# Padding the rows of the Q, K and gate-logit tiles to 256 bytes, and computing the gates' exp in place

## The chip, the cores and the metric

The kernel runs on one core of one Trainium2 chip. The metric is the device time of one execution, in microseconds (us). Most executions of one kernel on one chip lie within some 0.3% of each other.

## The reference, cut to what matters

A gated linear recurrence (8 heads of 48, 4 batches, 768 steps), then a mixture of four experts over the 3072 rows that come out of it.

```python
f = 1.0 / (1.0 + np.exp(-f_logit))
for t in range(S):                                  # S = 768
    state = f[:, :, t, :, None] * state + einsum('bhd,bhe->bhde', k[:, :, t], v[:, :, t])
    y[:, :, t] = einsum('bhd,bhde->bhe', q[:, :, t], state)
x = y.transpose(0, 2, 1, 3).reshape(3072, 384)
p = domain_probs / (domain_probs.sum(-1, keepdims=True) + 1e-09)
for e in range(4):                                  # w1: 384 x 1024, w2: 1024 x 384
    out += p[:, e:e + 1] * (np.maximum(x @ w1[e], 0.0) @ w2[e])
```

## The kernel before

The recurrence is done in 6 chunks of 128 steps. A small planner fixes the order of the instructions on every engine before anything is emitted, and puts 34 filler matmuls into gaps to keep the tensor engine's clock up. Inputs are loaded per chunk, in the first chunk one batch at a time: 128 partitions x 8 heads, thus 1024 rows of 48 floats (192 bytes) per load. Each of the inputs f (gate logits), q and k has four tiles, called slots here. A slot holds two batches: in chunk 0 batches 0 and 1 go to slot 0 and batches 2 and 3 to slot 1, chunk 1 uses slots 2 and 3, and so on around.

```python
shapes = {
    "f": ([T, 2 * H, D], FP32), "q": ([T, 2 * H, D], FP32), "k": ([T, 2 * H, D], FP32), ...
    "ex": ([T, 2 * H, D], FP32), ...                # T = 128, H = 8, D = 48
}
def load(c, nm, b, n):
    if (c, nm) == (0, "v"):                         # issued by GpSimd, casts to bf16
        ins[c, nm, b] = nc.gpsimd.dma_start(out=tl("vb", c, b), in_=srcs[nm][c, :, b * H:(b + n) * H, :])
        if b < 2:
            after(ins[c, nm, b], ins[v_gate[b]])    # v_gate = [(0, "k", 1), (0, "k", 2)]
        return
    ins[c, nm, b] = nc.sync.dma_start(out=tl(nm, c, b // 2)[:, hh(b, n), :], in_=srcs[nm][c, :, b * H:(b + n) * H, :])
    ...
def load_w(i, e, which, ks, cols):                  # weights, issued by GpSimd after v
    ...
    if i == w_last:
        after(ins["w", i], ins[1, "k", 0])

def gate1(c, b, n):
    nc.scalar.activation(out=tl("ex", c, b)[:, 0:n * H], in_=tl("f", c, b // 2)[:, hh(b, n), :], func=AF.Exp, scale=-1.0)
def gate2(c, b, n):
    ...
    nc.scalar.activation(out=g[:, hh(b, n), 0:D], in_=tl("ex", c, b)[:, 0:n * H], func=AF.Ln, bias=1.0)

# order of the first loads: letter and batch
"f0 k0 q0 f1 k1 q1 f2 f3 k2 q2 v0 k3 q3 v1 v2".split()
```

The v loads of the first chunk are issued by GpSimd only when the k loads of batches 1 and 2 have landed. And the weight pieces are issued on the same engine after the v loads, so a late k load of batch 2 delays the weights too.

Of the kernel before, what the change touches and what calls it, by code (L numbers as in the profile page):

```python
# [8 lines left out]
FP32 = mybir.dt.float32  # L9
BF16 = mybir.dt.bfloat16  # L10
AF = mybir.ActivationFunctionType
# [91 lines left out]
def kernel(  # L103
# [11 lines left out]
    nc = tc.nc  # L115
    B, H, S, D = q.shape
    assert (B, H, S, D) == (4, 8, 768, 48)
    T = 128
# [3 lines left out]
    P2 = 64  # L122
# [12 lines left out]
    wk = ctx.enter_context(tc.tile_pool(name="wk", bufs=1))  # L135
    PS = bass.MemoryType.PSUM
    ps = ctx.enter_context(tc.tile_pool(name="ps", bufs=1, space=PS))
    rooms = {"ps_m": 4, "ps_t": 4, "f": 4, "q": 4, "k": 4, "v": 4, "ex": 2, "gp": 4, "e": 3, "qk": 7,
             "vb": 7, "egs": 8, "QK": 4, "AT": 2, "yb": 2, "xT": 2, "h": 2, "o": 6}
    P = Plan(rooms)  # L140

# [13 lines left out]
    for nm, nb in (("gp", 2), ("qk", 2)):  # L155
        for i in range(rooms[nm]):
            t = pads[nm, i] = const.tile([T, nb, H, P2], BF16, name=f"{nm}{i}")
            nc.vector.memset(t[:, :, :, D:P2], 0.0)
    for i in range(rooms["e"]):
# [5 lines left out]
        out=mask01, in_=mask01, compare_op=ALU.is_ge, fill=0.0,  # L165
# [5 lines left out]
    for i in range(2):  # L171
        t = const.tile([MP, B, NP, 2 * D], BF16, name=f"sb{i}")
# [14 lines left out]
    for nm, a in (("f", f_logit), ("q", q), ("k", k), ("v", v)):  # L187
        srcs[nm] = a.rearrange("b h (c t) d -> c t (b h) d", t=T)
    ins = {}
    tiles = {}  # L190
    shapes = {
        "f": ([T, 2 * H, D], FP32), "q": ([T, 2 * H, D], FP32), "k": ([T, 2 * H, D], FP32), "v": ([T, 2 * H, D], FP32),
        "ex": ([T, 2 * H, D], FP32), "egs": ([128, 16], FP32), "vb": ([T, H, D], BF16),
        "QK": ([128, 2, NP, T], BF16), "AT": ([T, 2, NP, T], BF16), "yb": ([T, HD], BF16),
        "xT": ([128, KD, NT], BF16), "h": ([128, KF, NT], BF16), "o": ([128, Din], FP32),
        "cs": ([T, 512], FP32), "tp": ([128, 2, NP, T], BF16), "A": ([T, NP, T], FP32), "y": ([T, 512], FP32),
# [3 lines left out]
    def tl(kind, *key):  # L200

        if (kind, key) not in tiles:
            room = kind if kind in rooms else "ps_m" if kind in ("hp", "op", "pp") else "ps_t"
            slot = P.slot[(room, kind) + key if room.startswith("ps_") else (room,) + key]
            if room in ("gp", "qk", "e"):
                tiles[kind, key] = pads[room, slot]
            else:
                shape, dt = shapes[kind]
                pool = ps if room.startswith("ps_") else wk
                tiles[kind, key] = pool.tile(shape, dt, name=f"{room}{slot}")  # L210
        return tiles[kind, key]

    def after(later, earlier):
# [7 lines left out]
    def hh(b, n=1):  # L221
        return slice((b % 2) * H, (b % 2 + n) * H)

    def copy(eng, out, in_):
        if eng == "ACT":
            nc.scalar.copy(out=out, in_=in_)  # L226
        else:
            engines[eng].tensor_copy(out=out, in_=in_)
# [33 lines left out]
        nc.vector.tensor_tensor(out=pn, in0=tl("pp"), in1=psm.unsqueeze(1).broadcast_to([T, E, NR]), op=ALU.mult)  # L262

    def gate1(c, b, n):
        nc.scalar.activation(out=tl("ex", c, b)[:, 0:n * H], in_=tl("f", c, b // 2)[:, hh(b, n), :], func=AF.Exp, scale=-1.0)  # L265

    def gate2(c, b, n):
        g = tl("gp", c, b // 2).rearrange("t b h d -> t (b h) d")
        nc.scalar.activation(out=g[:, hh(b, n), 0:D], in_=tl("ex", c, b)[:, 0:n * H], func=AF.Ln, bias=1.0)  # L269

    def pe_cs(c, b):
        g, cs = tl("gp", c, b // 2)[:, b % 2], tl("cs", c, b)
# [134 lines left out]
    ld = {}  # L407
# [15 lines left out]
    for i, x in enumerate("f0 k0 q0 f1 k1 q1 f2 f3 k2 q2 v0 k3 q3 v1 v2".split()):  # L423
        nm, b = x[0], int(x[1])
# [30 lines left out]
    def attention(c, slot, gran):  # L455
        G, X, Y, GS, ET, VB = {}, [], [], [], {}, {}
        more = c < C - 1
        for b0 in range(0, B, gran):
            p, d, half = slot(b0, 0) - 0.5, 0.43 if gran == 1 else 0.84, b0 // 2
            g1 = P.add(f"gate1 {c}.{b0}", {"ACT": d}, lambda e, b0=b0: gate1(c, b0, gran), p,  # L460
                       deps=[ld[c, "f", b0 + i] for i in range(gran)], takes=[("ex", c, b0)], frees=[("f", c, half)])
            g2 = P.add(f"gate2 {c}.{b0}", {"ACT": d}, lambda e, b0=b0: gate2(c, b0, gran), p + 0.1,
                       deps=[g1], takes=[("gp", c, half)], frees=[("ex", c, b0)])
            for b in range(b0, b0 + gran):
                G[b] = g2
        for b in range(B):
            s = lambda k: slot(b, k)
            half = b // 2
# [4 lines left out]
                       deps=[G[b]], takes=[pt_("cs")], lag=0.2, frees=[("gp", c, half)])  # L473
            ex = P.add(f"exps {c}.{b}", {"ACT": 0.98 if c else 0.82}, on(exps), s(0) + 0.1, deps=[cs],
                       takes=[("e", c, b)] + ([("egs", c, b)] if c == 0 else []), frees=[pt_("cs")])
            GS.append(P.add(f"egs {c}.{b}", {"POOL": 0.8}, on(dma_egs), s(10), deps=[ex], takes=[("egs", c, b)],
                            frees=[("e", c, b)], lag=2.8) if c and more else None)
            pe = {"DVE": 0.47} if c == 0 and b == B - 1 else {"DVE": 0.47, "POOL": 1.36} if c == 0 else None
            qm = P.add(f"q {c}.{b}", pe or ({"DVE": 0.8} if (c, b) < (1, 2) else {"POOL": 1.1}), one(product, 0), s(4) - 0.2,
                       deps=[ex, ld[c, "q", b]], takes=[("qk", c, b)], frees=[("q", c, half), ("e", c, b)])  # L480
            km = P.add(f"k {c}.{b}", pe or ({"DVE": 0.5} if (c, b) < (1, 2) else {"POOL": 1.0}), one(product, 1), s(4) - 0.1,
                       deps=[ex, ld[c, "k", b]], takes=[("qk", c, b)], frees=[("k", c, half), ("e", c, b)])
            vb = ld[0, "v", b] if c == 0 else P.add(f"v {c}.{b}", {"POOL": 0.5, "ACT": 0.52} if c == 1 else {"POOL": 0.5}, one(cast_v), s(4),
                       deps=[ld[c, "v", b]], takes=[("vb", c, b)], frees=[("v", c, half)])
            if (c, b) < (1, 2):
                tq = P.add(f"tpq {c}.{b}", {"PE": 0.22}, on(pe_tp, 0), s(4), deps=[qm],
                           takes=[pt_("tp")], frees=[("qk", c, b)], lag=0.2)
                tk = P.add(f"tpk {c}.{b}", {"PE": 0.22}, on(pe_tp, 1), s(4) + 0.01, deps=[km],
                           takes=[pt_("tp")], frees=[("qk", c, b)], lag=0.2)
                parts = [(slice(0, 2), [tq, tk])] if c or b < B - 1 else [(slice(j, j + 1), [tj]) for j, tj in enumerate((tq, tk))]  # L490
                et = [P.add(f"ev_tp {c}.{b}", {"DVE": 0.69, "ACT": 1.05} if c else {"DVE": 0.6, "ACT": 0.92} if len(parts) == 1 else {"DVE": 0.35, "ACT": 0.49},
                            lambda e, b=b, js=js: copy(e, tl("QK", c, b)[0:MP, js], tl("tp", c, b)[0:MP, js]), s(4) + 0.1,
                            deps=ds, takes=[("QK", c, b)], frees=[pt_("tp")]) for js, ds in parts]
            else:
                et = [P.add(f"tp {c}.{b}", {"DMA": 1.8}, on(dma_tp), s(4), deps=[qm, km], takes=[("QK", c, b)],
                            frees=[("qk", c, b)], lag=2.5)]
# [4 lines left out]
        for bs in pairs:  # L501
            at = P.add(f"at {c}.{bs[-1]}", {"PE": 0.43 if len(bs) == 1 else 0.66}, lambda e, bs=bs: [pe_at(c, b) for b in bs], slot(bs[-1], 7),
                       deps=[t for b in bs for t in ET[b]], takes=[("ps_t", "A", c, b, r) for b in bs for r in range(2)], lag=0.2,
                       frees=[("QK", c, b) for b in bs])
            for b in bs:
                AT_[b] = at
        for b in range(B):
# [3 lines left out]
            at, vb = AT_[b], VB[b]  # L511
            eA = [P.add(f"ev_at{r} {c}.{b}", {"DVE": 0.7 if c else 0.62}, on(ev_at, r), s(7) + 0.1 + 0.1 * r, deps=[at],
                        takes=[("AT", c, b)], frees=[pt_("A", r)]) for r in range(2)]
            y = P.add(f"y {c}.{b}", {"PE": 0.4 if c else 0.28}, on(pe_y), s(11), deps=eA + [vb, kvdone.get((c - 1, b))],
                      takes=[pt_("y")], frees=[("QK", c, b), ("AT", c, b), ("vb", c, b)], lag=0.2)
# [4 lines left out]
                        lambda e, b=b, ks=ks: copy(e, tl("yb", c, b)[:, cs_(ks)], tl("y", c, b)[:, cs_(ks)]), s(11) + 0.1,  # L520
                        deps=[y], takes=[("yb", c, b)], frees=[pt_("y")]) for ks in parts]
            if (c, b) < (1, 2):
                xdone[c, b] = []
                for ks, eyk in zip(parts, ey):
                    xt = P.add(f"xt {c}.{b}", {"PE": 0.17}, on(pe_xt, ks), s(13), deps=[eyk],
                               takes=[pt_("xp", ks.start)], frees=[("yb", c, b)], lag=0.2)
                    xdone[c, b].append(
                        P.add(f"ev_xt {c}.{b}", {"ACT": 0.48, "DVE": 0.4} if c else {"ACT": 0.4, "DVE": 0.3} if len(parts) == 1 else {"ACT": 0.3, "DVE": 0.25},
                              lambda e, b=b, ks=ks: copy(e, tl("xT", c)[:, ks, b * T:(b + 1) * T], tl("xp", c, b, ks.start)[:, ks]),
                              s(13) + 0.1, deps=[xt], takes=[("xT", c)], frees=[pt_("xp", ks.start)]))  # L530
            else:
                xdone[c, b] = [P.add(f"xt {c}.{b}", {"DMA": 0.9}, on(dma_xt), s(13), deps=ey, takes=[("xT", c)],
                                     frees=[("yb", c, b)], lag=2.2)]
            X.append(xdone[c, b])
        for b in range(B if more else 0):
# [4 lines left out]
                       takes=[pt_("KV")], frees=[("vb", c, b), ("qk", c, b)], lag=0.2)  # L540
            ek = P.add(f"ev_kv {c}.{b}", {"DVE": 0.74}, on(ev_kv), s15 + 0.1,
                       deps=[kv, kvdone.get((c - 1, b))], frees=[pt_("KV")])
            kvdone[c, b] = P.add(f"state {c}.{b}", {"POOL": 1.75}, on(state), s15 + 0.2,
                                 deps=[ek, GS[b]], frees=[("egs", c, b)])
# [17 lines left out]
    def add_o(c, e, nt, half):  # L562
# [9 lines left out]
        if half == 1 or by_cols:  # L572
# [4 lines left out]
            if e == E - 1:  # L577
                P.add(f"store {c}.{nt}.{part}", {"DMA": 0.6}, lambda _: store(c, nt, cols), p - 25, deps=[ev], frees=[("o", c, nt)])

    attention(0, lambda b, s: -200 + 3.6 * b + s * 0.8, 1)  # L580
    pl = P.add("ld p", {"DMA": 0.2}, lambda e: load_p(), -989.5, lag=3.0)
    pp = P.add("pp", {"PE": 0.6}, lambda e: pe_pp(), -1, deps=[pl], takes=[("ps_m", "pp")], lag=0.2)
# [17 lines left out]
    for c in range(C):  # L600
        u0 = unit[0]
        if c + 1 < C:
            base = u0 + {0: 10, 1: 0}.get(c, -6)
            attention(c + 1, lambda b, s, base=base: base + 2 + 5 * b + s, 2)
        if c + 2 < C:
            for half in range(2):
                for j, nm in enumerate("fkqv"):
                    add_load(c + 2, nm, 2 * half, 2, u0 + {0: 38}.get(c, 30) + 4 * half + j, deps=wd[3, 1])
        if c == 0:

            for fcs, n0, n1, xs, nf in ((range(0, KF // 2), 0, N2, LO, 1), (range(0, KF // 2, 2), N2, NT - T, [2], 2),
                                        (range(KF // 2, KF), 0, NT - T, LO + [2], 1), (range(0, KF, 4), NT - T, NT, [3], 4)):
                zip_units([(c, 0, fc, n0, n1, xs, nf) for fc in fcs], [])
            unit[0] = u0 + 2 * KF
        elif c == 1:
            zip_units([], ol(0, E - 1, ALL))
            zip_units(hl(c, 0, 0, N2, LO), [])
            for e in range(1, E):
                zip_units(hl(c, e, 0, N2, LO), ol(c, e - 1, LO))
            zip_units(hl(c, 0, N2, NT, HI), ol(c, E - 1, LO))  # L620
            for e in range(1, E):
                zip_units(hl(c, e, N2, NT, HI), ol(c, e - 1, HI))
            zip_units(hl(c + 1, 0, 0, NT, ALL), ol(c, E - 1, HI))
        elif c == 2:
            pass
        else:
            zip_units(hl(c, 0, 0, NT, ALL), ol(c - 1, E - 1, ALL))
        for e in range(E if c == 1 else 1, E):
            zip_units(hl(c, e, 0, NT, ALL), ol(c, e - 1, ALL))
# [6 lines left out]
    t = 2.5  # L636
# [42 lines left out]
```

## Time and profile before

| | before |
|---|---|
| time, median (lowest to highest) | 298.65 us (298.17 to 298.88), 3 runs |
| span in the profile | 296.6 us |
| tensor engine busy | 289.0 us |
| share of queue q1 (f, q, k, v and stores) in 16 DMA engines' time | 52.0% |
| k load of batch 2, issue to landing | 3.89 us |
| k load of chunk 1 that the last weight piece waits for | 7.75 us |

### The profile page before, as it was taken

Reading aid. Unit: us, or ns where it says so; the run is one execution under the profiler, and the core shown is the slowest. Engines: PE = TensorE matmul, PEld = TensorE weight load, DVE = VectorE, ACT = ScalarE, POOL = GpSimd, SP = SyncE. Lnnn points to the kernel's source line nnn. Section 1 sums busy time; section 2 is a strip of 40 time slices with the busy share of each in tenths; the row PEclk is TensorE's granted clock in tenths of the full one; section 3 lists DMA queues with packets and bytes.
Section 4 is the critical chain, followed back from the end, with each engine's and each line's share of the span. In section 5 each row is a group of like instructions: output and inputs, shape, how many; then the busy total and the mean of one; then the engine's idle time right before and its main releaser. Section 6 shows DMA issues by size and latency. Waiting matters only on the chain.

```text
span 296.6 us, 5591 instructions
## 1 busy us (share of the span) xinstructions
PE 289.0 (97%) x2172; PEld 170.0 (57%) x2172; DVE 126.1 (43%) x250; ACT 174.3 (59%) x317; POOL 106.1 (36%) x180
## 2 busy tenths in 40 slices
PE   6899999999999999999999999999999999999995
PEld 2476555567777775555555555555555555555553
DVE  6786012785763673045375235243523222101223
ACT  5656656666684667777477575554475544465440
POOL 5786401138767448144449372243220000000000
PEclk9999999999999999999999999999999999999999
DMA  7999999998979999998979932102432100200002
GB/s 157 200 169 206 207 192 210 189 210 167 201 152 166 191 171 185 209 187 164 198 133 218 179 60 35 27 0 67 122 61 30 27 2 27 80 2 0 0 2 106
DMA packets 136462, 36.43 MB, mean 123 GB/s; under 512 B 126812, under 2 KB 135644, under 8 KB 136436
## 3 DMA queue, kind: packets, MB, share of 16 engines
q1 hardware_dynamic: 125188, 29.35, 52.0%
q0 software_dynamic: 11248, 6.72, 16.4%
q8 instruction: 17, 0.28, 0.4%
q14 instruction: 9, 0.07, 0.1%
HBM read 31.51 MB, written 4.72 MB: 122 GB/s over the span
## 4 chain that ended last, share of the span: by engine, by line
PE 78%; DMA 14%; POOL 3%; SPq 2%; issue 1%; ACT 1%; DVE 0%; POOLq 0%
PE ps_m L389 37%; PE ps_m L374 35%; DMA w_sb<-in_moe_w_dram 10%; DMA k<-in_k_dram 4%; SPq L237 2%; POOL w_sb L246 2%; PE ps_t L325 2%; PE ps_t L340 1%; PE ps_t L336 1%; PE ps_t L273 1%; POOL vb L233 1%; PE ps_t L346 1%; ACT e L293 1%; DVE o L396 0%; ACT xT L226 0%
## 5 line engine op out<-in xcount | busy, mean ns | idle before, releaser
L385 ACT ACTIVATE h<-ps_m 128x512 bf16<-128x512 f32 (+2 forms) x188 | 102.4, 548 | 91.9 <-PE ps_m L374 88.9
L374 PE MATMUL ps_m<-xT,w_sb 128*128 128x512 bf16 (+3 forms) x708 | 152.8, 339 | 0.6 <-ACT xT L226 0.6
L389 PE MATMUL ps_m<-w_sb,h 128*128 128x384 bf16 (+1 forms) x776 | 152.6, 324 | 0.1
L389 PEld LDWEIGHTS <-h 128*128 128x128 bf16 x776 | 75.0, 98 | 59.0 <-DMA w_sb<-in_moe_w_dram 0.3
L396 DVE SCALAR_TENSOR_TENSOR o<-ps_m,pn,o 128x384 f32<-128x384 f32 (+1 forms) x73 | 44.5, 612 | 117.3 <-PE ps_m L389 111.1
L374 PEld LDWEIGHTS <-w_sb 128*128 128x128 bf16 x708 | 65.3, 98 | 43.5 <-issue 0.7
L301 POOL TENSOR_TENSOR qk<-q,e 128x384 bf16<-128x384 f32 x18 | 21.4, 1195 | 36.5 <-ACT e L293 34.3
L360 POOL TENSOR_TENSOR Sf<-Sf,egs 48x192 f32<-48x192 f32 x40 | 20.2, 504 | 36.5 <-DVE Sf L353 34.4
L329 DVE TENSOR_TENSOR AT<-ps_t,mask 128x512 bf16<-128x512 f32 x48 | 30.2, 683 | 5.1 <-PE ps_t L325 5.1
L383 DVE TENSOR_SCALAR h<-ps_m 128x256 bf16<-128x256 f32 (+2 forms) x40 | 19.3, 499 | 26.5 <-PE ps_m L374 13.1
L293 ACT ACTIVATE e<-ps_t 128x384 f32<-128x384 f32 x48 | 26.7, 668 | 5.0 <-PE ps_t L273 3.5
L301 POOL TENSOR_TENSOR qk<-k,e 128x384 bf16<-128x384 f32 x20 | 20.2, 1013 | 8.7 <-ACT e L293 5.5
L353 DVE TENSOR_TENSOR Sf<-Sf,ps_t 48x192 f32<-48x192 f32 x40 | 14.0, 350 | 10.3 <-PE ps_t L346 9.4
L246 POOL DMA_DIRECT2D w_sb<-in_moe_w_dram x11 | 8.8, 807 | 18.5 <-DMA k<-in_k_dram 17.2
L361 POOL CAST sb<-Sf 48x192 bf16<-48x192 f32 x40 | 13.6, 340 | 2.6
L398 ACT ACTIVATE o<-ps_m,pn 128x384 f32<-128x384 f32 x22 | 12.8, 582 | 2.5 <-PE ps_m L389 1.5
L644 PE MATMUL ps_m<-busy 128*128 128x512 bf16 x34 | 10.9, 423 | 1.5 <-DVE busy L144 1.5
L265 ACT ACTIVATE ex<-f 128x768 f32<-128x768 f32 (+1 forms) x14 | 10.4, 746 | 1.8 <-DMA f<-in_f_logit_dram 1.8
L298 POOL DMA_DIRECT2D egs<-e x16 | 9.0, 563 | 6.9 <-ACT e L293 6.9
L340 PE MATMUL ps_t<-vb,AT 128*128 128x48 bf16 x192 | 11.4, 184 | 0.0
L269 ACT ACTIVATE gp<-ex 128x768 bf16<-128x768 f32 (+1 forms) x14 | 10.5, 751 | 0.3
L340 PEld LDWEIGHTS <-AT 128*128 128x128 bf16 x192 | 9.9, 97 | 1.1
(54 smaller groups left out, 120.6 us busy)
## 6 DMA issues: line engine op xcount, KB each, us to landing
out_dram<-o SPq DMA_DIRECT2D x23, 192.0 KB, 2.0
w_sb<-in_moe_w_dram POOLq DMA_DIRECT2D x5, 768.0 KB, 18.0
k<-in_k_dram SPq DMA_DIRECT2D x10, 384.0 KB, 5.6
q<-in_q_dram SPq DMA_DIRECT2D x10, 384.0 KB, 5.5
v<-in_v_dram SPq DMA_DIRECT2D x10, 384.0 KB, 5.7
f<-in_f_logit_dram SPq DMA_DIRECT2D x9, 384.0 KB, 4.6
w_sb<-in_moe_w_dram POOLq DMA_DIRECT2D x6, 384.0 KB, 9.0
f<-in_f_logit_dram SPq DMA_DIRECT2D x6, 192.0 KB, 3.8
```

The costliest lines, as they stand in the source:

```text
L246: ins["w", i] = nc.gpsimd.dma_start(out=w[:, e, ks, cols], in_=r[e][:, ks, cols])
L293: nc.scalar.activation(out=o, in_=i, func=AF.Exp, scale=1.0 if j else -1.0)
L301: engines[eng].tensor_tensor(out=tl("qk", c, b)[:, j, :, 0:D].rearrange("t (i r) d -> t i r d", r=2), in0=tl("qk"[j], c, b // 2)[:, hh(b), ...
L329: nc.vector.tensor_tensor(out=tl("AT", c, b)[:, r].rearrange("s i t -> s (i t)"), in0=tl("A", c, b, r).rearrange("s i t -> s (i t)"), in1= ...
L340: nc.tensor.matmul(out=y[:, h * D:(h + 1) * D], lhsT=AT[:, r, i, :], rhs=vb[:, h, :], start=(c == 0), stop=True, skip_group_check=True)
L353: nc.vector.tensor_tensor(out=Sf[rows, b], in0=Sf[rows, b], in1=KV[rows, :, r, :], op=ALU.add)
L360: nc.gpsimd.tensor_tensor(out=Sf[rows, b], in0=Sf[rows, b], in1=eg, op=ALU.mult)
L374: nc.tensor.matmul(out=hp(c, e, fc, n0, n1, nf)[:, f], lhsT=w1_sb[:, e, kk, (fc + f) * 128:(fc + f + 1) * 128], rhs=tl("xT", c)[:, kk, n0: ...
L383: nc.vector.tensor_relu(out=dst, in_=src)
L385: nc.scalar.activation(out=dst, in_=src, func=AF.Relu)
L389: nc.tensor.matmul(out=tl("op", c, e, nt, part)[:, cols], lhsT=tl("h", c, e, half_of(c, nt * T))[:, fc, nt * T:(nt + 1) * T], rhs=w2_sb[:, ...
L396: nc.vector.scalar_tensor_tensor(out=o, in0=op, scalar=pe, in1=o, op0=ALU.mult, op1=ALU.add)
```

## The change

The intent is to give each row of 192 bytes a block of 256 bytes of its own in the f, q and k tiles, and to save the two tiles that held the result of exp, which pays for part of the larger tiles.

```diff
-    rooms = {..., "v": 4, "ex": 2, "gp": 4, ...}
+    rooms = {..., "v": 4, "gp": 4, ...}
-        "f": ([T, 2 * H, D], FP32), "q": ([T, 2 * H, D], FP32), "k": ([T, 2 * H, D], FP32), ...
-        "ex": ([T, 2 * H, D], FP32), ...
+        "f": ([T, 2 * H, P2], FP32), "q": ([T, 2 * H, P2], FP32), "k": ([T, 2 * H, P2], FP32), ...   # P2 = 64
-                tiles[kind, key] = pool.tile(shape, dt, name=f"{room}{slot}")
+                t = pool.tile(shape, dt, name=f"{room}{slot}")
+                tiles[kind, key] = t[:, :, 0:D] if kind in ("f", "q", "k") else t
# gate1
-        nc.scalar.activation(out=tl("ex", c, b)[:, 0:n * H], in_=tl("f", c, b // 2)[:, hh(b, n), :], func=AF.Exp, scale=-1.0)
+        nc.scalar.activation(out=tl("f", c, b // 2)[:, hh(b, n), :], in_=tl("f", c, b // 2)[:, hh(b, n), :], func=AF.Exp, scale=-1.0)
# gate2
-        nc.scalar.activation(out=g[:, hh(b, n), 0:D], in_=tl("ex", c, b)[:, 0:n * H], func=AF.Ln, bias=1.0)
+        nc.scalar.activation(out=g[:, hh(b, n), 0:D], in_=tl("f", c, b // 2)[:, hh(b, n), :], func=AF.Ln, bias=1.0)
# the f slot is freed after ln instead of after exp
```

More of the change, by code (lines that the diff above doesn't have):

```diff
@@ L137 @@
     ps = ctx.enter_context(tc.tile_pool(name="ps", bufs=1, space=PS))
-    rooms = {"ps_m": 4, "ps_t": 4, "f": 4, "q": 4, "k": 4, "v": 4, "ex": 2, "gp": 4, "e": 3, "qk": 7,
+    rooms = {"ps_m": 4, "ps_t": 4, "f": 4, "q": 4, "k": 4, "v": 4, "gp": 4, "e": 3, "qk": 7,
              "vb": 7, "egs": 8, "QK": 4, "AT": 2, "yb": 2, "xT": 2, "h": 2, "o": 6}
@@ L191 @@
     shapes = {
-        "f": ([T, 2 * H, D], FP32), "q": ([T, 2 * H, D], FP32), "k": ([T, 2 * H, D], FP32), "v": ([T, 2 * H, D], FP32),
-        "ex": ([T, 2 * H, D], FP32), "egs": ([128, 16], FP32), "vb": ([T, H, D], BF16),
+        "f": ([T, 2 * H, P2], FP32), "q": ([T, 2 * H, P2], FP32), "k": ([T, 2 * H, P2], FP32), "v": ([T, 2 * H, D], FP32),
+        "egs": ([128, 16], FP32), "vb": ([T, H, D], BF16),
         "QK": ([128, 2, NP, T], BF16), "AT": ([T, 2, NP, T], BF16), "yb": ([T, HD], BF16),
@@ L460, in attention @@
             g1 = P.add(f"gate1 {c}.{b0}", {"ACT": d}, lambda e, b0=b0: gate1(c, b0, gran), p,
-                       deps=[ld[c, "f", b0 + i] for i in range(gran)], takes=[("ex", c, b0)], frees=[("f", c, half)])
+                       deps=[ld[c, "f", b0 + i] for i in range(gran)])
             g2 = P.add(f"gate2 {c}.{b0}", {"ACT": d}, lambda e, b0=b0: gate2(c, b0, gran), p + 0.1,
-                       deps=[g1], takes=[("gp", c, half)], frees=[("ex", c, b0)])
+                       deps=[g1], takes=[("gp", c, half)], frees=[("f", c, half)])
             for b in range(b0, b0 + gran):
```

## The prediction

> **What bounds the kernel now.** I read four views in this order: the page's busy shares, the busy time by stretch, the tensor engine's waits, and the chain of work that ended last.
>
> The page's first rows:
>
> ```profile
> PE 289.0 (97%) x2172; PEld 170.0 (57%) x2172; DVE 126.1 (43%) x250; ACT 174.3 (59%) x317; POOL 106.1 (36%) x180
> PE   6899999999999999999999999999999999999995
> DMA  7999999998979999998979932102432100200002
> ```
>
> The matmul row is full from the third slice on, and every other engine has 40% or more of its time free. The DMA row is full for the first half too, so two resources are candidates. The busy time of each engine by stretch (columns: stretch and length, then PE, PEld, DVE, ACT, POOL busy, clock, DMA share, GB/s) separates them:
>
> ```profile
> 0.00:7.40 7.40, 5.01 (x21) 1.86 (x22) 4.70 (x17) 4.32 (x8) 4.00 (x16) 1.00 0.79 157
> 7.40:14.80 7.40, 6.59 (x73) 3.49 (x72) 5.22 (x9) 5.04 (x14) 5.76 (x6) 1.00 1.50 201
> 14.80:22.20 7.40, 7.11 (x95) 5.21 (x95) 6.10 (x13) 4.41 (x10) 6.22 (x9) 1.00 1.38 168
> 22.20:44.50 22.30, 22.30 (x156) 12.95 (x153) 6.04 (x18) 13.79 (x25) 7.67 (x17) 1.00 1.23 202
> 44.50:60.00 15.50, 15.35 (x102) 8.55 (x101) 8.46 (x15) 10.33 (x19) 2.06 (x3) 1.00 1.15 202
> 60.00:90.00 30.00, 29.43 (x287) 21.71 (x285) 20.48 (x46) 20.10 (x40) 20.07 (x32) 1.00 0.95 183
> 90.00:210.00 120.00, 120.00 (x923) 70.75 (x921) 52.05 (x99) 75.11 (x136) 56.05 (x95) 1.00 0.77 137
> ```
>
> PE idles 2.39 us in the first stretch (7.40 - 5.01), then 0.81, 0.29, 0, 0.15, 0.57 and nothing from 90 to 210. What else it idles is the end of the program (the last matmul, evictions and stores). The granted clock is 1.00 in all of these. So the time is a fixed list of matmuls, plus a few idle microseconds before 90 us. The matmul waits with an engine as releaser:
>
> ```profile
> PE ps_m L644 <- DVE busy L144: 1.5, 1, 1.5
> PE ps_t L273 <- ACT gp L269: 0.8, 2, 0.4
> PE ps_t L310 <- DVE qk L301: 0.6, 1, 0.6
> PE ps_m L374 <- ACT xT L226: 0.6, 1, 0.6
> PE ps_t L310 <- ACT QK L226: 0.2, 1, 0.2
> ```
>
> The first is start-up (a memset before the warm-up matmuls). The next two hang on loads: gates wait for f, products for q. The chain of waits, as start, length and what, shows that DMA still paces the middle of the first 60 us:
>
> ```profile
> 20.53 21.10 DMA w_sb<-in_moe_w_dram
> ...
> 42.07 7.75 DMA k<-in_k_dram
> ...
> 50.37 8.82 DMA w_sb<-in_moe_w_dram
> 59.19 0.05 issue
> 59.24 1.47 PE ps_m L389 x8
> ```
>
> The last weight piece waits for one k load of chunk 1 and lands at 59.19, and PE takes it up at 59.24: just in time. A slower k load would stop PE there; a faster one gains almost nothing, since PE is fully busy before it.
>
> **What the Trainium skill says.** (1) "DMA: Bandwidth & Descriptors", section "How a descriptor splits into AXI transactions": a descriptor that starts 256-byte aligned goes out in pieces of 256 bytes plus a rest, and one that is not aligned starts its first piece at the boundary below, so that a 192-byte row may need one piece or two. Its examples are reads; for writes it is my inference. The trace neither confirms nor denies it, because in the kernel before every tile mixes all offsets. It shows only the rate: queue q1 moved its rows at about 230 GB/s in the saturated part of the first 7.4 us, thus 192 x 16 / 230 = 13.4 ns per row on each of 16 engines (estimate). (2) "ScalarE: Activation LUTs", section "What ACT_TABLE_LOAD costs": an activation with immediate operands takes 186 + 0.833 N ns whatever the function. The trace agrees: 506 by the formula and 520 and 523 measured for the 384-wide exp and ln, 826 against 837 and 842 for the 768-wide. Already before, ln writes 48-of-64 rows and exp flat ones, with no difference, so the pitch of an operand is free here on the write side. (3) "SBUF — State Buffer", Specifications: cachelines of 16 bytes. A 192-byte row that starts on a multiple of 64 is 12 whole lines at either pitch, so I expect no read penalty. The trace has no case of a padded fp32 row read from SBUF by ACT.
>
> **The change part by part.**
> *Pitch.* The number of bytes, rows and DMA issues is the same: only where a row lands changes. The evident intent is one aligned 256-byte block per row. I built both kernels and read the addresses that the allocator gave. Before, the twelve f, q and k tiles have pitch 192, and each has 8 of 16 rows across a 256-byte boundary: 96 of 192. After, the tiles start at 64, 128 or 192 modulo 256, since the pool doesn't align to 256. The six tiles of slots 0 and 2 start at 64, and a row fills [64, 256): none crosses. The six of slots 1 and 3 start at 128 or 192: all 16 rows cross. That is again 96 of 192. The sum is unchanged and only its order moves: the loads for batches 0 and 1 get easier, those for 2 and 3 harder.
> What that is worth at the most, counting 32-byte beats in the page's way: before (6 + 8 + 10 + 12) / 4 = 9 per row; after 8 in slots 0 and 2, and in slot 1 10 for f and 12 for k and q, mean 11.3. A load of batch 0 has 196.6 KB, at 230 GB/s 0.85 us. Six first loads: 6 x 0.85 x (8/9 - 1) = -0.57 us. Six second ones: 6 x 0.85 x (11.3/9 - 1) = +1.3 us. The sum is +0.7 us on the last q load, which the product at 13.3 us waited 0.67 us for. The source rows in HBM are unaligned as before, and if reading sets the rate (I think so, since it is not changed and no worse on average) all of this is zero. I take a third: -0.2 us on the two gate waits (0.8 us together), +0.2 us on the q wait: 0.
> *Chunk 1.* Its first half, with the k load in the chain, goes to slot 2, no crossings: if anything earlier, worth at most the 0.57 and 0.15 us of PE idle there. I take -0.1.
> *Exp in place.* It removes the two ex tiles, and no instruction: 14 exp and 14 ln remain. The f tile is held until ln ends, one or two instructions longer; at most 50.94 + 0.83 - 48.99 = 2.8 us from exp's start. The next load into that slot is issued at 97.0, and other slots have tens of microseconds as well, so no load waits. I compared the order of instructions of the two builds: with the tile's name replaced, it is the same on all five engines, every matmul and DMA issue in its place. The plan's 34 filler matmuls stay too.
> *Products.* POOL's q product takes 1195 ns and k's 1013, with the q side's e read at a 16-byte inner step: an inner step costs, and here the inner step stays at 4 bytes. I count 0 for the 48 products.
> Sum: 298.65 + 0 - 0.1 + 0 = about 298.5.
>
> **The rivals.** (a) The pitch works as meant and every row gets cheaper. For it: DMA is full for half the span. Against it: the addresses, and PE, which is what the time is made of. Its ceiling is all PE idle before 90 us but for start-up: 2.39 + 0.81 + 0.29 + 0.15 + 0.57 - 1.52 = 2.69 us, 0.9%; what I'd expect of it is 297.5. (b) Crossing rows write slower, and the loads for batches 2 and 3 become the wait: for it the 0.67 us wait for q; size +0.7 to +1.3 us, thus 299.3 to 300. (c) Padded reads slow ACT or POOL. 20% on the gates (10.4 + 10.5 us in all) would be 4 us on ACT, 41% free, of which only the first four pairs matter: 4 x 1.04 x 0.2 = 0.8 us. 20% on POOL's products (21.4 + 20.2 us) would be 8 us on an engine 64% free. PE had no wait from 90 to 210, so that is hidden too: 299.5. (d) Holding f turns into a load wait: excluded by the distances above.
>
> **Range and chances.** Runs of before spread by 0.7 us, and the rivals reach from 297.5 to 300. I put 8 in 10 on 297.4 to 299.7. Faster by 2% needs 6 us, and there are only 2.69 to take: 1%. Slower by 2% needs 6 us of new PE idle, four times rival (b): 1%. Within 2%: 98%.
>
> **What would show it.** In the profile after: PE busy within 1 us of 289; the same counts; exp and ln at 510 to 530 and 830 to 850 ns; POOL's products near 1195 and 1010; the chain of waits again through the weight pieces and k. Landing times of f, k and q loads of slots 0 and 2 shorter than of slots 1 and 3 would show that crossings count; equal ones, that reading sets the rate. I would be wrong if exp in place took much longer than 523 ns, if POOL's products passed 1.5 us, or if PE gained gaps after 90 us.

## More of the kernel before

The share of a DMA queue is the time that its packets took, over the time of the 16 DMA engines. At a fixed number of packets and bytes, as here, it measures how long a packet takes (over the span, which differs by up to 3% between the runs). It stands in the page's part on queues (packets, MB, share):

```profile
q1 hardware_dynamic: 125188, 29.35, 52.0%
```

What begins the chain of waits in the first 20 us is the k load of batch 2 (3.89 us from issue to landing) and, released by it, GpSimd's issue of the next v loads (start, length, what):

```profile
7.16 3.89 DMA k<-in_k_dram
11.35 1.83 POOL vb L233 x2
```

The tensor engine's matmuls of the experts begin at 19.75, without a wait. The columns are start, length, engine, line, operation, operands:

```profile
19.75 0.82 PE L374 MATMUL ps_m<-xT,w_sb 128*128 128x256 bf16 x6
```

An experiment is compared with the runs of the kernel before that were made beside it, on its chip.

## The result, and the profile after

Measured beside each other, four runs each: before 298.59 us (298.17 to 298.88), after 299.40 us (299.13 to 299.66). The ratio is 1.0025, with a 95% interval of 1.0011 to 1.0040. The change is within 2% of before, and it is slower by a quarter of a per cent, not faster by a hair.

The page's first row and the queue after:

```profile
PE 290.3 (97%) x2172; PEld 170.3 (57%) x2172; DVE 126.1 (42%) x250; ACT 174.2 (58%) x317; POOL 106.0 (36%) x180
...
q1 hardware_dynamic: 125188, 29.35, 56.5%
```

The counts are the same on every engine. DVE, ACT and POOL take the same time within 0.1 us. But the same 125188 packets and 29.35 MB took 56.5% of the DMA engines' time instead of 52.0%. The span is 297.9 us, 1.3 more than in the profile before. The busy time by stretch, in the columns of the prediction's table:

```profile
0.00:7.40 7.40, 5.42 (x18) 2.02 (x19) 4.70 (x17) 4.28 (x8) 4.00 (x16) 1.00 0.79 156
7.40:14.80 7.40, 6.48 (x72) 3.52 (x70) 4.62 (x8) 4.68 (x13) 4.73 (x5) 1.00 1.48 177
14.80:22.20 7.40, 6.73 (x84) 4.23 (x82) 5.78 (x11) 4.18 (x8) 6.61 (x10) 1.00 1.62 169
22.20:44.50 22.30, 22.21 (x170) 13.31 (x168) 7.02 (x20) 13.77 (x26) 8.27 (x18) 1.00 1.23 203
...
90.00:210.00 120.00, 120.00 (x925) 70.91 (x924) 51.97 (x98) 74.80 (x137) 57.17 (x96) 1.00 0.84 139
```

From 7.4 to 14.8 us the rate fell from 201 to 177 GB/s. From 14.8 to 22.2 the tensor engine's idle time rose from 0.29 to 0.67 us (7.40 - 6.73), and only 84 matmuls ended there instead of 95. From 90 to 210 us it is full in both. The loss is made before 25 us: the order of PE's 2172 matmuls is the same in both traces, and taken one by one they start 0.31 us later than before at 10 us, 1.16 later at 20, 1.42 at 25 and 1.34 at the end. The chain of waits and the first matmuls of the experts, after:

```profile
7.17 4.89 DMA k<-in_k_dram
12.37 1.81 POOL vb L234 x2
14.17 6.68 DMA w_sb<-in_moe_w_dram
```

```profile
20.90 0.83 PE L375 MATMUL ps_m<-xT,w_sb 128*128 128x256 bf16 x6 [0.38 <-DMA w_sb<-in_moe_w_dram]
```

The k load is issued at the same time, 7.16 and 7.17, and takes 4.89 us instead of 3.89. GpSimd's issue of v moves from 11.35 to 12.37, and the first weight piece behind it is issued at 14.17 and lands at 20.85. PE waits 0.38 us for it and starts the experts at 20.90 instead of 19.75. The square bracket is the idle time before the instruction and what ended it. A second, parallel path is q of the same batches: its product on the vector engine, before and then after:

```profile
13.28 0.56 DVE L301 TENSOR_TENSOR qk<-q,e 128x384 bf16<-128x384 f32 x1 [0.67 <-DMA q<-in_q_dram]
```

```profile
13.88 0.56 DVE L302 TENSOR_TENSOR qk<-q,e 128x384 bf16<-128x384 f32 x1 [0.74 <-DMA q<-in_q_dram]
```

One reading to avoid: the sum of PE's idle time before 90 us hardly grew, and its busy time grew by 1.3 us, as if there were more work. The fillers account for most of that (line, operation, count, busy us, mean ns; before, then after):

```profile
L644 PE MATMUL ps_m<-busy 128*128 128x512 bf16 x34 | 10.9, 423 | 1.5 <-DVE busy L144 1.5
```

```profile
L645 PE MATMUL ps_m<-busy 128*128 128x512 bf16 x34 | 12.0, 459 | 1.5 <-DVE busy L144 1.5
```

In this run five fillers that start at 5.14 us took 2.29 us, against 1.24 from 5.11 before. That is time in which PE would have waited for loads anyway. An experiment below ("swap") has the same loss with fillers of 423 ns, so they are not its cause.

### The profile page after: what moved, and what is told of

The parts are those of the page before. It is cut to its first block, busy times and chain, and to the rows that moved or that the text cites. A ratio compares the mean times of both kernels' runs of the same rounds, so it can differ in the third digit from the quotient of the medians. Undisturbed runs are those within 1.5% of the kernel's fastest.

```text
span 297.9 us, 5591 instructions
## 1 busy us (share of the span) xinstructions
PE 290.3 (97%) x2172; PEld 170.3 (57%) x2172; DVE 126.1 (42%) x250; ACT 174.2 (58%) x317; POOL 106.0 (36%) x180
## 3 DMA queue, kind: packets, MB, share of 16 engines
q1 hardware_dynamic: 125188, 29.35, 56.5%
## 4 chain that ended last, share of the span: by engine, by line
PE 91%; DMA 4%; SPq 2%; ACT 1%; POOL 1%; issue 1%; DVE 0%
PE ps_m L375 42%; PE ps_m L390 42%; DMA w_sb<-in_moe_w_dram 2%; SPq L238 2%; PE ps_t L326 2%; DMA k<-in_k_dram 2%; PE ps_t L341 1%; PE ps_t L337 1%; PE ps_t L347 1%; PE ps_t L274 1%; POOL vb L234 1%; ACT e L294 1%; PE ps_t L311 0%; PE ps_t L366 0%; DVE yb L229 0%
## 5 line engine op out<-in xcount | busy, mean ns | idle before, releaser
L645 PE MATMUL ps_m<-busy 128*128 128x512 bf16 x34 | 12.0, 459 | 1.5 <-DVE busy L144 1.5
L266 ACT ACTIVATE f<-f 128x768 f32<-128x768 f32 (+1 forms) x14 | 10.5, 749 | 4.5 <-DMA f<-in_f_logit_dram 4.4
L270 ACT ACTIVATE gp<-f 128x768 bf16<-128x768 f32 (+1 forms) x14 | 10.5, 750 | 0.3
```

## The experiments

The theory after the result: a row that lies across a 256-byte boundary of SBUF takes a DMA longer to write, and the change did not remove such rows but put them all into the loads of slots 1 and 3. The rivals: exp in place or the longer pitch as such costs the time; it doesn't matter which slots have the crossing rows; what counts is the number of beats of a row, not the number of pieces; and, for the size, that the loss is in slot 3 as well as in slot 1.

The tool for most of them is an unused pad tile that is allocated just ahead of a named slot. It shifts that slot and those behind it by so many floats:

```diff
+                if f"{room}{slot}" in PADS:
+                    wk.tile([T, PADS.pop(f"{room}{slot}")], FP32, name=f"pad_{room}{slot}")
                 t = pool.tile(shape, dt, name=f"{room}{slot}")
```

The tile starts modulo 256 were read from each build. With the pitch of 256, a start of 0 or 64 means that no row crosses (0 to 192, 64 to 256), and a start of 128 or 192 that all do. In the changed kernel slots 0 and 2 start at 64, and slots 1 and 3 at 128 or 192. All experiments gave correct results. Some of the texts name theories by letters; each gives the numbers that they expect of its run. Of the profiles, `cross192` alone has a short dip of the granted clock (0.992 on average).

### All tiles at one start: 0, 64, 192

```diff
 # align0:   every row within its block
+PADS = {'f0': 48, 'f1': 48, 'k1': 48, 'f2': 32, 'f3': 32}
 # align64:  the same with start 64
+PADS = {'f1': 48, 'k1': 48, 'f2': 32, 'f3': 32}
 # cross192: every row crosses
+PADS = {'f0': 32, 'f1': 48, 'k1': 48, 'f2': 32, 'f3': 32}
```

> The changed kernel, with five small pad tiles in the pool so that all twelve f, q and k tiles start at 0 modulo 256: no row crosses a 256-byte boundary. Theory A (a row that crosses costs DMA time, and the loads of batches 2 and 3 in the head carry all of the loss): about 298.0 us, faster than the kernel before by 0.5, the k load issued at 7.2 us lands in under 3.9 us instead of 4.89, and the first w1 matmul starts before 19.75 us instead of 20.90. Theory B (exp in place, or the longer hold of f, costs the time): still about 299.4. Theory C (the padded pitch itself is slow, whatever the start): 299.4 or more.

> As align0, but all twelve tiles start at 64 modulo 256, so each row fills bytes 64 to 256 of its block: no crossing, but no aligned start. If only crossing counts (A): the same as align0 within 0.3 us. If the start alignment counts, as the beats of the skill's page would have it (8 a row against 6): between align0 and the changed kernel, some 0.5 us over align0. B and C: 299.4.

> As align0, but all twelve tiles start at 192 modulo 256: all 192 rows cross. A: slower than the changed kernel, 300.5 to 301.5 us, and now the first loads too land later than in it (f of batch 0 at or after 3.6 us). B and C: 299.4.

Before, on the same chip: 298.47 us (11 runs). Measured:

| | time, us (runs) | ratio, 95% | q1 share | k load of batch 2 |
|---|---|---|---|---|
| align0 | 297.97 (6) | 0.9982, 0.9968 to 0.9997 | 48.9% | 3.53 us |
| align64 | 298.41 (5) | 0.9998, 0.9983 to 1.0012 | 49.1% | 3.54 us |
| cross192 | 304.86 (5) | 1.0202, 1.0180 to 1.0224 | 62.0% | 5.38 us |

The rate inside the saturated head shows the crossing without any inference from shares. It is the transfer view for 4.5 to 8.5 us, when only q1 is active; first before, then cross192:

```profile
DMA packets 4682, 0.88 MB, mean 221 GB/s; under 512 B 4682, under 2 KB 4682, under 8 KB 4682
```

```profile
DMA packets 3473, 0.66 MB, mean 164 GB/s; under 512 B 3473, under 2 KB 3473, under 8 KB 3473
```

Every packet here is one row of 192 bytes. 16 engines x 4.00 us / 4682 = 13.7 ns per row and engine before, where half of the rows cross, and 16 x 4.00 / 3473 = 18.4 ns where all do. In align0, where none does, it is 13.9 ns (4610 packets): no faster than before. The changed kernel has 4599 packets in this stretch (13.9 ns), which is mostly filled with the loads of slot 0 (the last of them, q of batch 1, lands at 8.10). From 9.5 to 10 us only loads of slot 1 are in flight there, and its rate is that of cross192, 16 x 0.50 / 436 = 18.3 ns:

```profile
DMA packets 436, 0.08 MB, mean 166 GB/s; under 512 B 436, under 2 KB 436, under 8 KB 436
```

The kernel before had 640 packets in that half microsecond.

So the crossing counts a good deal, and removing it gains next to nothing in time, although k landed earlier and the experts' first matmul started at 19.16 (align0) and 19.12 us (align64) instead of 19.75. In align64's trace the gain is lost again at 28.5 us, where PE waits 0.82 us for a weight piece. cross192 lost far more than the 300.5 to 301.5 us expected of it; whether it is slower by 2% is unclear (interval 1.0180 to 1.0224). It lost its 6.4 us in the steady state too: PE was busy 116.0 of the 120 us from 90 to 210 (117.0 in cross128 below, whose clock had no dip), part of it waiting for the transposing DMA that brings the experts' input:

```profile
167.54 6.38 PE L379 MATMUL ps_m<-xT,w_sb 128*128 128x512 bf16 x21 [2.04 <-DMA xT<-yb]
```

That is a different regime from the changed kernel, whose PE is full there.

### Exp in place without the pitch

```diff
-        "f": ([T, 2 * H, P2], FP32), "q": ([T, 2 * H, P2], FP32), "k": ([T, 2 * H, P2], FP32),
+        "f": ([T, 2 * H, D], FP32), "q": ([T, 2 * H, D], FP32), "k": ([T, 2 * H, D], FP32),
```

> The kernel before with exp written in place and no ex tiles, pitch 192 as before. A: the same as before, 298.6. B: 299.4. C: 298.6. Exp should take 520 and 837 ns as before.

298.63 us (298.18 to 299.47, 6 runs), ratio 1.0006 (0.9991 to 1.0020), q1 at 51.5%. The tiles are also taken whole again, as before (left out of the cut). Half of the rows cross, as before, the k load of batch 2 took 3.98 us, and the time is that of before. The in-place exp costs nothing that can be seen; the loss belongs to the pitch.

### Which slot: only slot 1, or only slot 3, put right

```diff
 # fix_slot1: f1, k1 and q1 start at 64; slot 3 still crosses
+PADS = {'f1': 48, 'k1': 48, 'f2': 32}
 # fix_slot3: f3, k3 and q3 start at 64; slot 1 still crosses
+PADS = {'f3': 32}
```

> The changed kernel with only the tiles of slot 1 (f1, k1, q1; batches 2 and 3 of the head) moved to 64 modulo 256 by pads; slot 3 still crosses in every row. Theory A1 (all of the loss comes from the six head loads of batches 2 and 3): 298.3 to 298.5 us, like the kernel with every tile at 64, and the k load issued at 7.2 us lands in about 3.5 us. Theory A2 (the loss is spread over all loads that cross, later chunks as well): about 299.0.

> The changed kernel with only slot 3 moved to 64 modulo 256; slot 1 still crosses. A1: 299.4, no gain, with the k load of batch 2 at 4.9 us as before. A2: about 298.9. The share of queue q1 should fall from 56.5% towards 53% in either case.

Before on that chip: 298.43 us. fix_slot1: 298.33 (297.94 to 299.90, 6 runs), ratio 0.9999 (0.9978 to 1.0020). fix_slot3: 299.40 (298.98 to 300.02, 6 runs), ratio 1.0027 (1.0013 to 1.0042). The shares of q1 are 52.1 and 51.8%: the two kernels have the same number of crossing rows, and the same share as before, yet one has the changed kernel's loss and the other shows none (the two intervals just overlap). fix_slot1's k load was expected in about 3.5 us and took 4.66. The chain of waits of fix_slot3 is that of the changed kernel:

```profile
7.06 5.00 DMA k<-in_k_dram
12.35 1.80 POOL vb L238 x2
14.16 6.71 DMA w_sb<-in_moe_w_dram
20.91 0.83 PE ps_m L379 x6
```

The loss of the changed kernel therefore hangs on slot 1, as far as intervals this wide can tell. Its loads in the first chunk are the ones that the chain shows; the same slot is used again in later chunks, where the tensor engine has no wait. One run each can be uneven, so fix_slot1 was run again on another chip:

> The same kernel as fix_slot1, because its profile fell on a run of 298.92 us, above its median of 298.33, with the k load of batch 2 at 4.66 us. If that was a stray run: again 298.3 +- 0.3, and now k in 3.4 to 3.9 us and the product waits less than 0.3 us for q. If slot 1's start does not set that load's time: k again over 4.5 us.

298.82 us (297.73 to 299.80, 6 runs), ratio 1.0003 (0.9978 to 1.0028) against a before of 298.46. The k load took 3.94 us, so the 4.66 was not repeated. The ratio held; the expected 298.3 and the product's expected short wait for q did not (0.63 us). On this chip both kernels scattered by 2 us. The traces separate the two kernels better than the times do: the experts' first matmul starts at 19.80 and 19.43 us in the two profiles of fix_slot1, and at 20.90, 20.88 and 20.91 where slot 1 crosses (the changed kernel, its repeat, fix_slot3).

### How many rows of a load cross: pitch of 224 bytes

```diff
-        "f": ([T, 2 * H, P2], FP32), "q": ([T, 2 * H, P2], FP32), "k": ([T, 2 * H, P2], FP32),
+        "f": ([T, 2 * H, 56], FP32), "q": ([T, 2 * H, 56], FP32), "k": ([T, 2 * H, 56], FP32),
```

Five rows of eight cross, mixed within each load.

> The changed kernel with a pitch of 224 bytes (56 floats): rows stay apart, no two adjoin, and 5 of 8 rows of each load cross, mixed with ones that do not. Theory M (a load pays for crossing only where crossings follow each other, since reading sets the pace of a mixed load): queue q1 near 53%, k of batch 2 near 4.0 us, time 298.4 to 298.9. Theory S (each crossing row costs the same, wherever it is: 13 points of q1 share for all rows, so 5/8 of that over 49%): q1 at 57%, k of batch 2 at 4.8 us, time 299.4 or more; the same if the kernel before was helped by rows that adjoin.

299.44 us (299.18 to 299.79, 4 runs), ratio 1.0030 (1.0017 to 1.0044); q1 at 54.4%, between the two expectations of 53 and 57; the k load took 4.41 us. The time was the one expected by S, the share by neither. What it gives is a third point: within one load the cost is not proportional to the share of crossing rows. With none, half, five eighths and all of them the share of q1 is 49, 52, 54.4 and 62%: half of the rows cost 3 points, the other half 10. It also tells against a rival, that rows which adjoin make crossing cheap in the kernel before: here none adjoin, and a share in proportion would be 57%. And it loses as much time as the changed kernel, though no load of it crosses as a whole.

### Pieces or beats: all tiles at 128

```diff
+PADS = {'f0': 16, 'f1': 48, 'k1': 48, 'f2': 32, 'f3': 32}
```

A row from 128 is cut by the boundary into 128 and 64 bytes, one from 192 into 64 and 128. If bytes fetched ahead of a start cost beats, as the Trainium skill tells of reads ("DMA: Bandwidth & Descriptors", section "How a descriptor splits into AXI transactions"), then a row from 192 has 12 beats of 32 bytes, one from 128 has 10, one from 64 has 8 and one from 0 has 6.

> All twelve tiles at 128 modulo 256: every row crosses, 128 bytes before the boundary and 64 after it (at 192 it was 64 and 128). If what counts is that a row goes out in two pieces: as with 192, 304 to 306 us and q1 near 62%. If the 32-byte beats of the skill's page count (10 a row against 12): clearly less, 300 to 302 us, q1 near 56%.

305.18 us (304.47 to 305.57, 4 runs), ratio 1.0219 (1.0202 to 1.0236); q1 at 62.9%, k in 5.4 us. It is no cheaper than cross192 (62.0%), and align0 and align64 are equal as well (48.9 and 49.1%). For these writes the number of pieces counts, and where in its block a row begins does not. (Between 0 and 64 that is shown less surely, since rows that do not cross may be held up by something other than writing, see below.)

### Crossing rows first: slots exchanged

```diff
+PADS = {'f0': 32, 'f1': 16, 'k1': 48}      # slots 0 and 2 at 192, slots 1 and 3 at 64
```

> The crossing slots swapped: slots 0 and 2 at 192 modulo 256, slots 1 and 3 at 64. The number of crossing rows is that of the changed kernel. If only the number counts: 299.4. If what counts is which loads stand on the head's path: in the head the first six loads are slow and push all the later ones, and the k load of chunk 1 that gates the last weights takes 8.5 us instead of 6.7: 299.6 to 300.5. The q1 share should be 56% either way.

299.44 us (298.95 to 299.67, 6 runs), ratio 1.0025 (1.0004 to 1.0046); q1 at 56.8%. PE now waits for the gates of the first batches (0.89 us at 5.16 and 1.03 at 8.79). The rate in slices of 0.25 us from 3 to 13 us, first the changed kernel, then swap, shows the crossing loads as a stretch near 160 in different places:

```profile
GB/s 232 223 235 216 204 237 227 238 234 255 169 152 224 214 187 209 253 223 199 229 260 202 214 230 194 176 170 163 145 151 150 143 154 151 147 156 164 186 175 160
```

```profile
GB/s 166 187 203 195 197 194 173 172 158 166 170 165 158 168 162 162 165 161 161 169 161 164 163 163 181 216 249 261 250 238 191 237 199 110 129 139 142 143 157 172
```

In swap it is 158 to 170 from 5 to 9 us, then 191 to 261 from 9.25 to 11 us, when the loads of slot 1 follow. In the changed kernel the fast stretch comes first, and from 9.25 us on it is 143 to 186. (From about 10 us in the changed kernel and 11 in swap the slices also hold v loads, which write 96-byte rows, so they don't measure crossing alone.) The size of the loss is the same within the noise: which of the two groups crosses does not matter for the time. The path does differ: matched one by one with those of before, swap's matmuls are 1.32 us late already at 10 us, from the two waits for gates. And swap's fillers took as long as before's (423 ns each), so slow fillers are not part of the loss.

### Repeats: the changed kernel, and align0

> The changed kernel itself once more, on whatever chip this falls, because the last three kernels ran on another chip where the kernel before scattered from 297.9 to 299.84 us. If the loss is real: a ratio of 1.001 to 1.004 again, k of batch 2 near 4.9 us, a q1 share near 56.5%, and a stretch of about 150 GB/s between 9.5 and 12 us. If it was scatter: a ratio within 0.999 to 1.001.

> The kernel with all tiles at 0 modulo 256 once more, for a narrower interval: 297.9 +- 0.3, a ratio to the kernel before of 0.997 to 0.9995; k of batch 2 in 3.5 us.

The changed kernel on a third chip: 299.71 us (299.18 to 300.35, 6 runs) against 299.16, ratio 1.0024 (1.0006 to 1.0042); q1 55.5%, k 4.99 us. The loss is real and of the same size. Its chain shows the later part as well, which answers to the prediction's fence of the chain before:

```profile
7.48 4.99 DMA k<-in_k_dram
...
21.97 21.33 DMA w_sb<-in_moe_w_dram
43.74 6.70 DMA k<-in_k_dram
50.98 9.63 DMA w_sb<-in_moe_w_dram
60.65 1.47 PE ps_m L390 x8
```

align0 on the second chip: 299.38 us (297.85 to 299.83, 6 runs) against 298.46, ratio 1.0017 (0.9988 to 1.0045), with q1 at 49.0% as in the first run. The gain of 0.2% that align0 had shown was not repeated, and neither was the k load of 3.5 us: it took 4.55, though no row crosses. Its profile has a fall of the rate to 121 to 145 GB/s around 6.5 to 7 us, which I can't explain. A late k load costs here as well (the experts' first matmul starts at 20.55 us, after a wait of 0.44 for its weights), so crossing rows are one cause of a late k load, not the only one, and a single profile cannot tell them apart. Over the twelve profiles without cross192 and cross128, k of batch 2 landed between 10.81 us (align0, span 296.2) and 12.47 (the repeat of the changed kernel, span 298.0), and the spans follow these landings (correlation 0.92). No version here is shown to beat the kernel before.

## Why the prediction was right or wrong

*The time.* 299.40 lies within the range of 297.4 to 299.7, near its upper end; the predicted 298.5 is 0.9 us too low, and the sign of the small change was wrong. The range held because it was drawn wide enough for rival (b), not because the sum behind the 298.5 was right.

*What held.* The kernel is bound by a fixed list of matmuls, and PE stayed full from 90 to 210 us. The ceiling put on any gain was right: even with no crossing row at all, the time moved by -0.5 us in one set of runs and +0.9 in the other. The addresses were right, and so was that the loads of batches 2 and 3 would get harder: f of batches 2 and 3 and k and q of batch 2 took 4.05, 4.29, 4.89 and 5.78 us from issue to landing, before 3.76, 3.90, 3.89 and 5.16, while f, k and q of batch 1 took 3.50, 3.57 and 3.50, before 3.63, 3.55 and 3.82. The in-place exp is free: ACT's exp and ln took 523 and 840 ns after, against 520 to 523 and 837 to 842 before. POOL's products did not change:

```profile
L302 POOL TENSOR_TENSOR qk<-q,e 128x384 bf16<-128x384 f32 x18 | 21.3, 1192 | 35.4 <-ACT e L294 33.2 <-issue 2.0
L302 POOL TENSOR_TENSOR qk<-k,e 128x384 bf16<-128x384 f32 x20 | 20.2, 1014 | 9.2 <-ACT e L294 5.5 <-ACT egs L296 3.1 <-POOL sb L362 0.4
```

No load waited for the f tile's longer hold, and the instruction order was the same. Rivals (a), (c) and (d) are out; (b), "the loads for batches 2 and 3 become the wait", with its 299.3 to 300, is what came.

*The step that failed.* It is this one: "if reading sets the rate (I think so, since it is not changed and no worse on average) all of this is zero. I take a third: -0.2 us on the two gate waits (0.8 us together), +0.2 us on the q wait: 0." Gain and loss were taken as two equal parts of one sum. The runs show that they are not equal. Rows that don't cross gain nothing in the head against a mixture of half and half (13.9 against 13.7 ns per row), and rows of loads in which every row crosses take a third longer (18.4 ns). A "third" was taken of both sides, where it was none of one and about all of the other. (The rate of about 230 GB/s in that estimate is 221 in the trace from 4.5 to 8.5 us; this changes its sums by less than 0.1 us.)

An estimate that ties the three rates together, from these numbers alone: if a row written in two pieces takes 18.4 ns, a piece takes 9.2, and a mixture of half and half 1.5 x 9.2 = 13.8 ns. That is just what the rows take when none crosses (13.9), which then is not the pace of writing but of something else, reading I suppose. In the kernel before, writing and reading would then be just in balance; grouping the crossing rows into whole loads breaks it on one side and gives nothing back on the other. This fits 5/8 as well: 1.625 x 9.2 = 15.0 ns, where the pitch of 224 had 14.5 (4401 packets). But rows that don't cross had 13.3 to 15.2 ns in this stretch of eight profiles, and half-crossing ones 13.4 and 13.7 in two, so that point decides nothing, and that reading is the other limit was argued, not shown.

*The size of the loss.* A load of one batch has 1024 rows, 64 per engine, so a load of crossing rows takes 64 x (18.4 - 13.7) = 0.30 us more. k of batch 2 is the third of these loads: 0.9 us by this estimate, and 1.00 measured (in the six profiles whose slot 1 does not cross, this load alone varied from 3.53 to 4.66 us, so the close fit is in part luck). q is the fourth: 1.2 us by it, but the product that waits for it moved by only 0.6 us (13.28 to 13.88). I leave that open; perhaps the v load, which is held back by k, competes with it less than before.

*The path that was missed.* The prediction named one victim, the product's wait for q. It did not see that k of batch 2 gates GpSimd's v issue and, through the same engine's order, the weights. That path brought +1.0 us from k, +1.02 at the v issue, and +1.15 at the first matmul of the experts; the medians moved by 0.8. The size that rival (b) gave (0.7 to 1.3 us) was right by both paths. The chain "again through the weight pieces and k" held in the second profile of the changed kernel; in the first the chain leaves the weights at 20.85 us and stays mostly on PE.

*Chunk 1, predicted -0.1.* In slot 2, where no row crosses now, the k load took 6.70 us instead of 7.75. That looks like the forecast gain, but the record doesn't show that crossing made it: in inplace_only the same tile has the same start modulo 256, half of its rows cross, and it took 6.7 us too (the issue's line in the transfer view, before and then inplace_only):

```profile
k<-in_k_dram SPq DMA_DIRECT2D x1, 384.0 KB, 7.8
```

```profile
k<-in_k_dram SPq DMA_DIRECT2D x1, 384.0 KB, 6.7
```

Over all profiles it took 6.69 to 6.99 us with no row crossing, 6.70 and 7.75 with half, 7.54 with five eighths, and 7.92 to 8.54 with all. So loads with five eighths or all of their rows crossing were longer here; what made the one of before long stays open. In the changed kernel the shorter load bought nothing, since everything ahead of it is 1 us late. In align0, where nothing was late, the weight piece behind it gave two thirds of the gain back:

```profile
42.07 6.74 DMA k<-in_k_dram
49.34 9.52 DMA w_sb<-in_moe_w_dram
58.91 1.47 PE ps_m L394 x8
```

The load is 1.01 us shorter, the weight piece behind it 0.70 longer (9.52 against 8.82), and PE goes on at 58.91 instead of 59.24. That is one trace: in align64 and inplace_only the same piece took 8.84 and 8.88.

## What to carry to other kernels

A pitch of 256 bytes does not align rows if the tiles do not start on 256 bytes: read the tile's address from the build, and count how many rows cross a boundary in each load, not only in the sum. Loads with half of their rows crossing were as fast here as loads with none, and loads of nothing but crossing rows took a third longer, so moving easy and hard rows apart can lose even where their number stays the same. And before padding anything, look at what the transfer would release: here even perfect alignment gave no gain that a second set of runs repeated, since the matmuls fill the time, while one load that is late by 1 us holds back everything that is issued behind it.

## What the Trainium skill lacked or had wrong

- "DMA: Bandwidth & Descriptors", section "How a descriptor splits into AXI transactions", gives examples of reads only, and says that the bytes before an unaligned start cost beats. For the writes of 192-byte rows into SBUF here only the number of pieces counted: q1 took 48.9 and 49.1% for starts of 0 and 64, and 62.0 and 62.9% for starts of 192 and 128. The number of pieces is the one that the section's rule gives.
- No page says that rows in one piece and rows in two pieces, mixed half and half in one load, can be as fast as rows in one piece alone (13.7 and 13.9 ns per row and engine, from 4.5 to 8.5 us, with no other queue active), while a load of nothing but crossing rows takes 18.4 ns.
- No page says that tiles of a pool may start anywhere modulo 256, so that a padded pitch alone doesn't keep rows within a block: the twelve tiles of the changed kernel start at 64, 128 and 192, and 96 of their 192 rows per partition cross.
